# GpSimd's sums and copies moved in its queue, and the seven products of the second FFN layer in a new order

## Chip, cores, metric

Each run uses one core of a Trainium2 chip. The metric is the device time of one execution in microseconds; medians of several runs are quoted.

## The reference

Attention with a threshold (8 batches, 8 heads, 576 positions, head size 64), whose output rows are the input of an FFN with ELU (512 to 2048 to 512):

```python
scores = scale * np.matmul(q, k.transpose(0, 1, 3, 2))
thresh = np.max(scores, axis=-1, keepdims=True) - tau
scores = np.where(scores >= thresh, scores, -1000000000.0)
attn = np.exp(scores - np.max(scores, axis=-1, keepdims=True))
attn = attn / (np.sum(attn, axis=-1, keepdims=True) + 1e-09)
x = np.matmul(attn, v)               # heads side by side: (4608, 512)
h = x @ w_in
g = np.where(h > 0.0, h, np.exp(np.minimum(h, 0.0)) - 1.0)
return g @ w_out
```

## The kernel before

All is float32. Heads go in pairs; a pair has five steps i0 to i4 (i4 holds the last 64 queries of both heads). From pair 7 on, a hand-ordered loop weaves each attention step with `QUOTA` half units of the FFN, so that TensorE (PE) always has matmuls while the other engines do the softmax. An FFN chunk (256 tokens) has 8 units of the first layer and 7 products of the second: 30 halves in ten steps. So the loop repeats every two pairs, called A (odd pairs) and B (even pairs).

The second layer multiplies 2x2 blocks with 7 products instead of 8, so GpSimd (POOL) makes 16 sums `s` of the activations per chunk, and the weights have sums `t`. Products gather in three places X, Y, Z of PSUM (the memory that matmuls write), and VectorE (DVE) adds places and kept tiles afterwards.

```python
def prep_q(pr):                                   # prep_k likewise, with one copy
    qT = qkp.tile([P, S], FP32, name="qT")
    nc.vector.transpose(qT, ...)
    qd = qds[pr % NQD]
    for i in range(2):
        nc.gpsimd.tensor_copy(qd[r, ...], qT[r, MAIN:])     # POOL waits for the transposition
# ...
def exponentials(pr, i, hs):
    nc.vector.tensor_reduce(st["mx"], ...)                  # maximum, reads PSUM
    nc.gpsimd.tensor_scalar(st["nb"], st["mx"], ...)        # bias
    nc.gpsimd.tensor_scalar(st["th"], st["mx"], ...)        # threshold
    nc.scalar.activation(e, ..., AF.Exp, bias=st["nb"])     # one for each head
# masks: DVE, w = (scores >= th) * e, frees the scores' PSUM (one buffer); then 1/sum into rs
# normalize: POOL, w = w * rs
# a first-layer unit ends with exp (ACT), minus one (POOL), elu (DVE)
# ...
QUOTA = ((2, 2), (2, 2), (2, 0), (2, 1), (2, 0))
for n in range(SWITCH, len(steps) + 3):
    # ...
    scores(*step)
    finish_units(after, slice(0, 2))        # exp, minus of the halves of the last step
    exponentials(*step)
    finish_units(after, slice(2, None))     # their elu and other DVE work
    run_extra(1.6)                          # two sums
    turn_squares(*steps[n - 1])
    after = ffn_halves(QUOTA[n % NB][0])
    masks(*step)
    (prep_q if i == 2 else prep_k)(pr + 1)  # only i2, i3
    finish_units(after, slice(0, None))     # exp, minus, elu of these halves
    normalize(*step)
    run_extra(1.6)                          # two sums more
    # ...
    after = ffn_halves(QUOTA[n % NB][1])
```

Each engine is given its instructions in the order of this text, and the timelines below show POOL and DVE run them in that order.

Of the kernel before, what the change touches and what calls it, by code (L numbers as in the profile page):

```python
# [9 lines left out]
FP32 = mybir.dt.float32  # L10
# [3 lines left out]
ALU = mybir.AluOpType  # L14
# [4 lines left out]
def kernel(  # L19
# [10 lines left out]
    nc = tc.nc  # L30
    PSUM = bass.MemoryType.PSUM
    P = 128
    B, H, S, D = q.shape
    DM, DF = moe_w_in.shape
    NC = S // P
    MAIN = NC * P
    TAIL = S - MAIN
# [14 lines left out]
    qkp = ctx.enter_context(tc.tile_pool(name="qkp", bufs=2))  # L52
# [5 lines left out]
    epool = ctx.enter_context(tc.tile_pool(name="epool", bufs=1))  # L58
# [8 lines left out]
    first = ExitStack()  # L67
# [28 lines left out]
    NQD, NVD = 2, 2  # L96
    qds = [const.tile([P, P], FP32, name=f"qd{i}") for i in range(NQD)]
# [51 lines left out]
    raws, pairs = {}, {}  # L149


    def load(pr, parts=("qm", "km", "v")):
        b, j = divmod(pr, NPAIR)
        tiles = raws.setdefault(pr, {})
        for name, src in (("qm", q), ("km", k)):
            if name not in parts:
                continue
            m = tiles[name] = raw.tile([P, S // T, T], FP32, name=name)
            for i in range(2):
                for d in range(2):  # L160
                    r = (2 * i + d) * T
                    nc.sync.dma_start(
                        m[r : r + T],
                        src[b, 2 * j + i].rearrange("(j t) d -> t j d", t=T)[:, :, d * T : (d + 1) * T],
                    )
        if "v" not in parts:
            return
        vm = tiles["vm"] = raw.tile([P, 2, NC, D], FP32, name="vm", bufs=2)
        vd = tiles["vd"] = vds[pr % NVD]
        for i in range(2):  # L170
            vh = v[b, 2 * j + i]
            nc.sync.dma_start(vm[:, i], vh[:MAIN].rearrange("(c p) d -> p c d", p=P))
            r = slice(i * TAIL, (i + 1) * TAIL)
            nc.sync.dma_start(vd[r, r], vh[MAIN:])

    def prep_q(pr):
        qT = qkp.tile([P, S], FP32, name="qT")
        nc.vector.transpose(qT, raws[pr]["qm"].rearrange("p j d -> p (j d)"))
        qd = qds[pr % NQD]
        for i in range(2):  # L180
            r = slice(i * D, (i + 1) * D)
            nc.gpsimd.tensor_copy(qd[r, i * TAIL : (i + 1) * TAIL], qT[r, MAIN:])
        pairs[pr] = [qT, None, qd]

    def prep_k(pr):

        kT = pairs[pr][1] = qkp.tile([P, TAIL + S], FP32, name="kT")
        nc.vector.transpose(kT[:, TAIL:], raws[pr]["km"].rearrange("p j d -> p (j d)"))
        nc.gpsimd.tensor_copy(kT[D:, :TAIL], kT[D:, S:])

    wTs, xts, open_steps, turns = {}, {}, {}, {}

# [161 lines left out]
    PLAIN = 2  # L354
    HM = DM // 2
    gs, ss, cur = {}, {}, {}
    extra = deque()

    def run_extra(budget):
        while extra and extra[0][0] <= budget:  # L360
            cost, _, f = extra.popleft()
            budget -= cost
            f()

    def need_extra(c):
        while any(x[1] <= c for x in extra):
            extra.popleft()[2]()
# [63 lines left out]
    def store(c, i, ot):  # L431
        g, hf = divmod(c, 2)
        t0 = hf * CT + i * P
        if g < B:
            nc.sync.dma_start(out[g * S + t0 : g * S + t0 + P, :], ot)
        else:
            for o in range(2):
                b0 = (t0 // TAIL + o) * S + MAIN
                nc.sync.dma_start(out[b0 : b0 + TAIL, :], ot[o * TAIL : (o + 1) * TAIL])

    def ffn2_plain(c, i, part):
# [10 lines left out]
        def done():  # L452
# [3 lines left out]
            if (c, i) == (PLAIN - 1, 1):  # L456
# [3 lines left out]
        return [lambda: run(0), lambda: run(1)], (done, lambda: None, lambda: None) if 4 * part + 4 == NFT else ()  # L460


    ORDER = ((("g", 0, 0), ("w", 0, 0), "X", True), (("s", 1), ("t", 0), "Y", True), (("s", 0), ("w", 0, 1), "Z", True),
             (("g", 1, 0), ("w", 1, 0), "X", False), (("s", 2), ("t", 1), "Y", False), (("s", 3), ("w", 1, 1), "Z", False),
             (("g", 1, 1), ("t", 2), "Y", False))

    def ffn2(c, m):
        left, right, place, begins = ORDER[m]

        def part(k):  # L470
            if left[0] == "s" or right[0] == "t":
                need_extra(c)
            if begins and k == 0:
                cur[c, place] = psum["f"].tile([P, 512], FP32, name="po", tag="f")[:, :HM]
            for u in range(k * NU // 2, (k + 1) * NU // 2):
                lhs = gs[c][:, u, left[1], left[2]] if left[0] == "g" else ss[c][:, left[1], u]
                if right[0] == "w":
                    rhs = w_out_sb[:, right[1] * NU + u, right[2] * HM : (right[2] + 1) * HM]
                else:
                    rhs = late["t"][:, right[1], u]  # L480
                nc.tensor.matmul(cur[c, place], lhs, rhs, start=(begins and u == 0), stop=(u == NU - 1),  # L481
                                 skip_group_check=True)

        def add(out, x, y):
            nc.vector.tensor_tensor(out, cur[c, x], cur[c, y], ALU.add)

        def kept(name, cols=HM, bufs=1):
            cur[c, name] = epool.tile([P, cols], FP32, name=name[:2], bufs=bufs)
            return cur[c, name]

        def first():
            nc.scalar.copy(kept("s1"), cur[c, "X"])

        def fourth():
            nc.scalar.copy(kept("ot0", DM, 2)[:, :HM], cur[c, "X"])

        def fifth():
            add(kept("ot1", DM, 2)[:, HM:], "Y", "t5")

        def sixth():  # L500
            add(cur[c, "ot0"][:, HM:], "Z", "u2")
            store(c, 0, cur[c, "ot0"])

        def seventh():
            add(cur[c, "ot1"][:, :HM], "Y", "s1")
            store(c, 1, cur[c, "ot1"])

        by_vector = {1: lambda: add(kept("u2"), "Y", "s1"), 2: lambda: add(kept("t5"), "Z", "s1"),
                     4: fifth, 5: sixth, 6: seventh}
        no = lambda: None  # L510
        posts = (no, no, by_vector[m]) if m in by_vector else (first if m == 0 else fourth, no, no)
        return [lambda: part(0), lambda: part(1)], posts

    units = deque()
# [9 lines left out]
    NP = B * NPAIR  # L524
# [10 lines left out]
    def heads_of(i):  # L535
        return [0, 1] if i < NC else [0]
# [33 lines left out]

    def ahead(pr, i):
        if i == 2 and pr + 1 < NP:
            prep_q(pr + 1)
            prep_k(pr + 1)
        if i == 3 and pr + 2 < NP:
            load(pr + 2, ("qm", "km"))
        if i == 3 and pr + 1 < NP and pr:
            load(pr + 1, ("v",))

    load(0)  # L580
    prep_q(0)
    prep_k(0)
    load(1)

    heads = [(pr, i, [h]) for pr, i in steps[:per_seq] for h in heads_of(i)]
# [28 lines left out]
    for n in range(per_seq, SWITCH):  # L614
        pr, i = steps[n]
# [29 lines left out]
    with tc.manual_schedule():  # L645
        after = []
        for n in range(SWITCH, len(steps) + 3):
            step = (*steps[n], heads_of(steps[n][1])) if n < len(steps) else None
            if SWITCH + 1 < n <= len(steps) + 1:
                fetch(*steps[n - 2])  # L650
            if step:
                scores(*step)
            finish_units(after, slice(0, 2))
            if step:
                exponentials(*step)
            finish_units(after, slice(2, None))
            run_extra(1.6)
            if SWITCH < n <= len(steps):
                turn_squares(*steps[n - 1])
            after = ffn_halves(QUOTA[n % NB][0])  # L660
            if step:
                masks(*step)
                pr, i = steps[n]
                if pr + 1 < NP and i in (2, 3):
                    (prep_q if i == 2 else prep_k)(pr + 1)
            finish_units(after, slice(0, None))
            if step:
                normalize(*step)
            run_extra(1.6)
            if n - 3 >= SWITCH:  # L670
                behind(*steps[n - 3])
            if step and pr + 2 < NP and i in (3, 4):
                load(pr + 2, ("qm",) if i == 3 else ("km",))
            if step and pr + 1 < NP and i == 3:
                load(pr + 1, ("v",))
            after = ffn_halves(QUOTA[n % NB][1])
        finish_units(after, slice(0, None))
        xts[B] = xpool.tile([P, KJ, MAIN], FP32, name="xt")
        nc.sync.dma_start(xts[B], xtail.rearrange("j p n -> p j n"))
        push_ffn(B)  # L680
        while pending or units:
            finish_units(ffn_halves(1), slice(0, None))
            run_extra(99)
# [32 lines left out]
```

## Time and profile before

| | before |
|---|---|
| time, median of the first 3 runs | 1466.87 us (1463.84 to 1468.86) |
| loop and tail, from the second step's scores of the loop to the end | 1189.3 us |
| a loop period (ten steps), mostly | 77.08 us |
| PE idle in a period | 1.15 us |

How to read a line: it gives start and length in us, then engine, line of the kernel, operation, tile written and tiles read, and in brackets the engine's idle time before it and who ended it. ACT is ScalarE, PEld the weight loads of PE, SPq the queue that issues DMAs. The tiles are `sc` scores, `mx` their maximum, `nb` bias, `th` threshold, `e` exponentials, `w` masked and normalized weights, `g` FFN activations, `po` products.

The prediction shows lines of waits: who waited for whom, us in total, times, longest. One view more, three of the waits of POOL in the period from 686.78 to 763.86 us (who waited for whom, us in total, times, longest):

```profile
POOL w L246 <- DVE rs L240: 10.0, 6, 3.6
POOL kT L189 <- DVE kT L188: 8.4, 2, 4.2
POOL qd L182 <- DVE qT L178: 6.9, 2, 4.2
```

### The profile page before, as it was taken

The page shows a single profiled execution, that of the slowest core. Times are in us where ns is not written, and L with a number is a line of the kernel's source. Part 1 is how long each engine was busy: PE and PEld are TensorE (multiplying, and loading weights), DVE is VectorE, ACT ScalarE, POOL GpSimd, SP SyncE. Part 2 cuts the span into 40 slices and gives each one's busy share as a digit, 9 for nine tenths or more (in the row PEclk, how much of TensorE's full clock was granted, in tenths as well). Part 3 has the DMA queues.
Part 4 walks back from the last instruction along what each step waited for, and adds up shares of the span by engine and source line. Part 5 has one row for each costly group of instructions (what it writes and reads, how often), then busy time and mean ns, then how long its engine had stood idle before and what let it go on. Part 6 is the DMA issues. An engine that isn't in the chain of part 4 may idle for free.

```text
span 1464.2 us, 20305 instructions
## 1 busy us (share of the span) xinstructions
PE 1396.0 (95%) x6822; PEld 1039.2 (71%) x6822; DVE 875.6 (60%) x1894; ACT 437.7 (30%) x780; POOL 671.3 (46%) x1194
## 2 busy tenths in 40 slices
PE   7988789999999999999999999999999999999998
PEld 4555535647777777777777777777777777888887
DVE  5887665566676766776666767676767674111111
ACT  4665544323232322222232223222322232101100
POOL 4665554446454453535362535353545444323422
PEclk9999999999999999999999999999999999999999
DMA  4244442176767667666676767666767665100000
GB/s 94 71 92 115 116 123 84 50 193 180 185 172 198 172 189 189 188 182 184 178 195 175 188 182 191 181 184 182 193 179 185 187 182 150 44 15 8 8 15 15
DMA packets 298904, 205.45 MB, mean 140 GB/s; under 512 B 206384, under 2 KB 270384, under 8 KB 298800
## 3 DMA queue, kind: packets, MB, share of 16 engines
q1 hardware_dynamic: 298800, 204.15, 52.6%
q8 instruction: 54, 0.88, 0.2%
q14 instruction: 50, 0.41, 0.1%
HBM read 119.87 MB, written 84.21 MB: 139 GB/s over the span
## 4 chain that ended last, share of the span: by engine, by line
PE 71%; DVE 12%; POOL 8%; ACT 3%; issue 3%; DMA 2%; SPq 1%; DVEq 0%; POOLq 0%; ACTq 0%
PE po L481 25%; PE ph L383 25%; PE sc L210 10%; PE pv L337 6%; DVE w L237 4%; POOL w L246 2%; ACT e L225 2%; POOL wtop L141 2%; PE po L449 2%; PE pv L333 2%; DVE mx L220 1%; PE rt L249 1%; DVE x L297 1%; POOL g L394 1%; DVE g L398 1%
## 5 line engine op out<-in xcount | busy, mean ns | idle before, releaser
L383 PE MATMUL ph<-xt,w_in_sb 128*128 128x256 f32 x2304 | 520.4, 382 | 3.2 <-DVE w_in_sb L145 3.2
L383 PEld LDWEIGHTS ph<-xt,w_in_sb 128*128 128x128 f32 x2304 | 432.6, 190 | 83.4 <-issue 21.0
L225 ACT ACTIVATE e<-sc,nb,keep 128x576 f32<-128x576 f32 x288 | 227.8, 829 | 514.6 <-POOL nb L221 513.5
L220 DVE TENSOR_REDUCE mx<-sc 128x2 f32<-128x1152 f32 (+1 forms) x176 | 199.8, 1136 | 188.2 <-PE sc L210 187.9
L246 POOL TENSOR_SCALAR w<-w,rs 128x576 f32<-128x576 f32 x288 | 220.1, 774 | 152.3 <-DVE rs L240 143.2
L237 DVE SCALAR_TENSOR_TENSOR w<-sc,th,e 128x576 f32<-128x576 f32 x288 | 226.8, 815 | 98.3 <-ACT e L225 57.4
L210 PE MATMUL sc<-kT,qT 64*128 64x288 f32 x1024 | 182.1, 441 | 20.1 <-DVE w L237 10.6
L398 DVE SCALAR_TENSOR_TENSOR g<-g,ph 128x512 f32<-128x512 f32 x144 | 97.9, 680 | 150.8 <-POOL g L394 150.8
L297 DVE STREAM_TRANSPOSE x<-w 128x512 f32<-128x512 f32 (+1 forms) x350 | 181.4, 567 | 1.1 <-POOL w L246 0.9
L394 POOL TENSOR_SCALAR g<-g 128x512 f32<-128x512 f32 x144 | 89.9, 625 | 199.2 <-ACT g L391 197.1
L210 PEld LDWEIGHTS sc<-kT,qT 64*128 64x128 f32 x1024 | 100.4, 191 | 87.3 <-issue 53.8
L391 ACT ACTIVATE g<-ph 128x512 f32<-128x512 f32 x144 | 86.0, 597 | 245.0 <-PE ph L383 243.6
L221 POOL TENSOR_SCALAR nb<-mx,nkeep 128x2 f32<-128x2 f32 (+1 forms) x176 | 52.6, 299 | 167.6 <-DVE mx L220 158.4
L481 PE MATMUL po<-w_out_sb,g 128*128 128x256 f32 x512 | 123.6, 383 | 3.4 <-DVE g L398 3.4
L481 PE MATMUL po<-t,s 128*128 128x256 f32 x512 | 118.9, 381 | 0.0
L481 PE MATMUL po<-w_out_sb,s 128*128 128x256 f32 x512 | 118.7, 381 | 0.0
L481 PEld LDWEIGHTS po<-w_out_sb,g 128*128 128x128 f32 x512 | 95.5, 190 | 24.8 <-DVE g L398 7.8
L481 PEld LDWEIGHTS po<-t,s 128*128 128x128 f32 x512 | 96.3, 190 | 17.2 <-issue 4.2
L481 PEld LDWEIGHTS po<-w_out_sb,s 128*128 128x128 f32 x512 | 96.4, 190 | 16.9 <-issue 4.2
L414 POOL TENSOR_TENSOR s<-g 128x256 f32<-128x256 f32 x128 | 93.2, 728 | 14.3 <-DVE g L398 12.9
L337 PE MATMUL pv<-wTb,vm 128*64 128x320 f32 x512 | 76.7, 439 | 0.0
L449 PE MATMUL po<-w_out_sb,g 128*128 128x512 f32 x128 | 62.4, 619 | 4.9 <-DVE w_out_sb L145 4.7
(63 smaller groups left out, 1088.5 us busy)
## 6 DMA issues: line engine op xcount, KB each, us to landing
there<-x SPq DMA_DIRECT2D x500, 144.0 KB, 3.1
wTb<-there SPq DMA_DIRECT2D x75, 576.0 KB, 4.4
wTa<-there SPq DMA_DIRECT2D x50, 576.0 KB, 3.7
qm<-in_q_dram SPq DMA_DIRECT2D x128, 72.0 KB, 2.7
km<-in_k_dram SPq DMA_DIRECT2D x128, 72.0 KB, 3.5
vm<-in_v_dram SPq DMA_DIRECT2D x64, 128.0 KB, 2.5
wst<-in_moe_w_in_dram SPq DMA_DIRECT2D x16, 512.0 KB, 4.2
wst<-in_moe_w_out_dram SPq DMA_DIRECT2D x16, 512.0 KB, 3.8
```

The source lines that it names most:

```text
L210: nc.tensor.matmul(scs[h][:, a, :HALF], qs[r], kT[r, k0 : k0 + HALF], start=True, stop=True)
L220: nc.vector.tensor_reduce(st["mx"][:, cs], src[:, :, :, :HALF], axis=AX.XY, op=ALU.max)
L225: nc.scalar.activation(e, st[h][:, :, :HALF], AF.Exp, bias=st["nb"][:, h : h + 1], scale=keep)
L237: nc.vector.scalar_tensor_tensor(wv, sc[:, :, :HALF], st["th"][:, h : h + 1], e, ALU.is_ge, ALU.mult, accum_out=sm[:, h : h + 1])
L246: nc.gpsimd.tensor_scalar(wv, wv, st["rs"][:, h : h + 1], 1.0, ALU.mult, ALU.mult)
L297: nc.vector.transpose(x[:, :, c0 : c0 + nc_], src.rearrange("p (c g n) -> p g c n", c=nc_, n=T))
L337: nc.tensor.matmul(pv[h * D : (h + 1) * D, g0 * T : g1 * T], vm[:, h, c], wT[:, g0:g1, h * (NC + 1) + c], start=False, stop=(c == NC - 1), ...
L383: nc.tensor.matmul(loc["ph"][:, k], w_in_sb[:, j, ft * P : (ft + 1) * P], xts[g][:, j, hf * CT : (hf + 1) * CT], start=(j == 0), stop=(j = ...
L394: nc.gpsimd.tensor_scalar(loc["g"], loc["g"], 1.0, -1.0, ALU.mult, ALU.add)
L398: nc.vector.scalar_tensor_tensor(loc["g"], loc["g"], 0.0, loc["h"], ALU.min, ALU.max)
L414: nc.gpsimd.tensor_tensor(out, x, y, op)
L481: nc.tensor.matmul(cur[c, place], lhs, rhs, start=(begins and u == 0), stop=(u == NU - 1), skip_group_check=True)
```

## The change

The intent: the bias and the threshold, on which the exponentials wait, shall not stand behind sums or copies in POOL's queue; and since sums then come later, the products that need none shall come first. Cut to its core:

```diff
     def prep_q(pr):
         nc.vector.transpose(qT, ...)
-        for i in range(2):
-            nc.gpsimd.tensor_copy(qd[...], qT[...])
+    def copy_q(pr):          # copy_k likewise
+        for i in range(2):
+            nc.gpsimd.tensor_copy(qd[...], qT[...])
@@ products: left, right, place, begins
-    ORDER = ((g00, w00, X, True), (s1, t0, Y, True), (s0, w01, Z, True), (g10, w10, X, False),
-             (s2, t1, Y, False), (s3, w11, Z, False), (g11, t2, Y, False))
+    ORDER = ((g00, w00, X, True), (g11, t2, Z, True), (g10, w10, X, False), (s1, t0, Y, True),
+             (s0, w01, Z, True), (s2, t1, Y, False), (s3, w11, Z, False))
@@ adds behind the products (DVE; a plain copy is on ACT)
+    0: s1 = X   1: w1 = Z + s1   2: out = X   3: u2 = Y + s1   4: t5 = Z + s1
+    5: out = Y + t5, out = Y + w1   6: out = Z + u2
@@ loop
             finish_units(after, slice(2, None))
-            run_extra(1.6)
+            run_extra(3.0)                      # three sums
             ...
             normalize(*step)
-            run_extra(1.6)
+            (copy_q if i == 2 else copy_k)(pr + 1)      # only i2, i3
```

(Product numbers count from 0, so `u2` is read behind product 3. The old adds are left out; the new ones are one more a chunk, which is why DVE has 1910 instructions after and 1894 before.)

More of the change, by code (lines that the diff above doesn't have):

```diff
@@ L178, in prep_q, with prep_k @@
         nc.vector.transpose(qT, raws[pr]["qm"].rearrange("p j d -> p (j d)"))
-        qd = qds[pr % NQD]
+        pairs[pr] = [qT, None, qds[pr % NQD]]
+    def prep_k(pr):
+        kT = pairs[pr][1] = qkp.tile([P, TAIL + S], FP32, name="kT")
+        nc.vector.transpose(kT[:, TAIL:], raws[pr]["km"].rearrange("p j d -> p (j d)"))
+    def copy_q(pr):
+        qT, _, qd = pairs[pr]
         for i in range(2):
@@ L182, in prep_q, with copy_k, prep @@
             nc.gpsimd.tensor_copy(qd[r, i * TAIL : (i + 1) * TAIL], qT[r, MAIN:])
-        pairs[pr] = [qT, None, qd]
-    def prep_k(pr):
-        kT = pairs[pr][1] = qkp.tile([P, TAIL + S], FP32, name="kT")
-        nc.vector.transpose(kT[:, TAIL:], raws[pr]["km"].rearrange("p j d -> p (j d)"))
+    def copy_k(pr):
+        kT = pairs[pr][1]
         nc.gpsimd.tensor_copy(kT[D:, :TAIL], kT[D:, S:])
+    def prep(pr):
+        for f in (prep_q, copy_q, prep_k, copy_k):
+            f(pr)
     wTs, xts, open_steps, turns = {}, {}, {}, {}
@@ L460, in ffn2_plain @@
         return [lambda: run(0), lambda: run(1)], (done, lambda: None, lambda: None) if 4 * part + 4 == NFT else ()
-    ORDER = ((("g", 0, 0), ("w", 0, 0), "X", True), (("s", 1), ("t", 0), "Y", True), (("s", 0), ("w", 0, 1), "Z", True),
-             (("g", 1, 0), ("w", 1, 0), "X", False), (("s", 2), ("t", 1), "Y", False), (("s", 3), ("w", 1, 1), "Z", False),
-             (("g", 1, 1), ("t", 2), "Y", False))
+    ORDER = ((("g", 0, 0), ("w", 0, 0), "X", True), (("g", 1, 1), ("t", 2), "Z", True), (("g", 1, 0), ("w", 1, 0), "X", False),
+             (("s", 1), ("t", 0), "Y", True), (("s", 0), ("w", 0, 1), "Z", True), (("s", 2), ("t", 1), "Y", False),
+             (("s", 3), ("w", 1, 1), "Z", False))
     def ffn2(c, m):
@@ L470, in part @@
         def part(k):
-            if left[0] == "s" or right[0] == "t":
+            if left[0] == "s":
                 need_extra(c)
-            if begins and k == 0:
+            if right[0] == "t":
+                need_extra(PLAIN)
+            if begins and k == 0 and (c, place) not in cur:
                 cur[c, place] = psum["f"].tile([P, 512], FP32, name="po", tag="f")[:, :HM]
@@ L482, in part, with finals, kept, post @@
                                  skip_group_check=True)
-        def add(out, x, y):
-            nc.vector.tensor_tensor(out, cur[c, x], cur[c, y], ALU.add)
-        def kept(name, cols=HM, bufs=1):
-            cur[c, name] = epool.tile([P, cols], FP32, name=name[:2], bufs=bufs)
-            return cur[c, name]
-        def first():
-            nc.scalar.copy(kept("s1"), cur[c, "X"])
-        def fourth():
-            nc.scalar.copy(kept("ot0", DM, 2)[:, :HM], cur[c, "X"])
-        def fifth():
-            add(kept("ot1", DM, 2)[:, HM:], "Y", "t5")
-        def sixth():
-            add(cur[c, "ot0"][:, HM:], "Z", "u2")
-            store(c, 0, cur[c, "ot0"])
-        def seventh():
-            add(cur[c, "ot1"][:, :HM], "Y", "s1")
-            store(c, 1, cur[c, "ot1"])
-        by_vector = {1: lambda: add(kept("u2"), "Y", "s1"), 2: lambda: add(kept("t5"), "Z", "s1"),
-                     4: fifth, 5: sixth, 6: seventh}
+        def finals(i, cols, x, y):
+            if (c, i) not in cur:
+                cur[c, i] = epool.tile([P, DM], FP32, name="ot", bufs=2), []
+            ot, done = cur[c, i]
+            if y is None:
+                nc.scalar.copy(ot[:, cols], cur[c, x])
+            else:
+                nc.vector.tensor_tensor(ot[:, cols], cur[c, x], cur[c, y], ALU.add)
+            done.append(cols)
+            if len(done) == 2:
+                store(c, i, ot)
+        def kept(name, x, y):
+            cur[c, name] = epool.tile([P, HM], FP32, name=name)
+            if y is None:
+                nc.scalar.copy(cur[c, name], cur[c, x])
+            else:
+                nc.vector.tensor_tensor(cur[c, name], cur[c, x], cur[c, y], ALU.add)
+        lo, hi = slice(0, HM), slice(HM, DM)
+        f, args = ((kept, ("s1", "X", None)), (kept, ("w1", "Z", "s1")), (finals, (0, lo, "X", None)),
+                   (kept, ("u2", "Y", "s1")), (kept, ("t5", "Z", "s1")), (None, ()), (finals, (0, hi, "Z", "u2")))[m]
+        def post():
+            if f:
+                f(*args)
+            else:
+                finals(1, hi, "Y", "t5")
+                finals(1, lo, "Y", "w1")
         no = lambda: None
-        posts = (no, no, by_vector[m]) if m in by_vector else (first if m == 0 else fourth, no, no)
+        posts = (post, no, no) if m in (0, 2) else (no, no, post)
         return [lambda: part(0), lambda: part(1)], posts
@@ L572, in ahead @@
         if i == 2 and pr + 1 < NP:
-            prep_q(pr + 1)
-            prep_k(pr + 1)
+            prep(pr + 1)
         if i == 3 and pr + 2 < NP:
@@ L580 @@
     load(0)
-    prep_q(0)
-    prep_k(0)
+    prep(0)
     load(1)
@@ L668 @@
                 normalize(*step)
-            run_extra(1.6)
+                if pr + 1 < NP and i in (2, 3):
+                    (copy_q if i == 2 else copy_k)(pr + 1)
             if n - 3 >= SWITCH:
```

## The prediction

> **What bounds the kernel now.** I read the page first, then windows, waits, timelines and single records, each time to ask whether TensorE (PE) stands still and for whom.
>
> ```profile
> PE 1396.0 (95%) x6822; PEld 1039.2 (71%) x6822; DVE 875.6 (60%) x1894; ACT 437.7 (30%) x780; POOL 671.3 (46%) x1194
> PE 71%; DVE 12%; POOL 8%; ACT 3%; issue 3%; DMA 2%; SPq 1%; DVEq 0%; POOLq 0%; ACTq 0%
> ```
>
> PE bounds it. The change touches only the hand-scheduled loop (attention of 125 steps woven with the FFN, about 262 to 1228 us) and the FFN tail behind it. The loop repeats every 10 steps: two pairs of heads, called A and B, of five steps i0 to i4, with one FFN chunk of 30 half units. Windows of one loop period and of two pieces of the tail (columns: length, then busy PE, PEld, DVE, ACT, POOL):
>
> ```profile
> 686.78:763.86 77.08, 75.93 (x385) 57.40 (x385) 53.16 (x116) 21.41 (x36) 35.91 (x69) 1.00 0.69 184
> 1303.90:1331.52 27.62, 27.62 (x129) 24.31 (x129) 5.24 (x8) 4.18 (x7) 12.71 (x19) 1.00 0.03 10
> 1331.52:1355.70 24.18, 24.18 (x114) 21.29 (x113) 2.39 (x5) 1.34 (x3) 3.44 (x5) 1.00 0.03 12
> ```
>
> The tail has no PE idle, so nothing is to be won there. A period has 1.15 us. Who makes PE (and its weight loads) wait over ten periods (378 to 1150 us):
>
> ```profile
> PE sc L210 <- DVE w L237: 8.7, 10, 0.9
> PE po L481 <- DVE g L398: 3.4, 11, 0.6
> PEld po L481 <- DVE g L398: 7.8, 11, 1.0
> PEld po L481 <- DVE ot L485: 2.7, 10, 0.3
> ```
>
> So two stalls a period, always at the same place: the scores of step A-i4 wait for the mask of A-i3 (which frees their PSUM), and the last two matmuls of product 0 wait for the last ELU of the chunk. The timelines of POOL, DVE and PE there:
>
> ```profile
> 753.38 0.53 POOL L182 COPY qd<-qT 64x64 f32<-64x64 f32 x2 [2.70 <-DVE qT L178]
> 754.00 0.62 POOL L394 TENSOR_SCALAR g<-g 128x512 f32<-128x512 f32 x1
> 754.60 1.47 POOL L246 TENSOR_SCALAR w<-w,rs 128x576 f32<-128x576 f32 x2
> 756.03 0.72 POOL L414 TENSOR_TENSOR s<-g 128x256 f32<-128x256 f32 x1
> 756.71 0.72 POOL L414 TENSOR_TENSOR s<-g,s 128x256 f32<-128x256 f32 x1
> 757.42 0.26 POOL L221 TENSOR_SCALAR nb<-mx,nkeep 128x2 f32<-128x2 f32 x1
> 755.26 1.35 DVE L220 TENSOR_REDUCE mx<-sc 128x2 f32<-128x1152 f32 x1
> 758.32 1.89 PE L481 MATMUL po<-w_out_sb,g 128*128 128x256 f32 x8
> 761.07 1.21 PE L210 MATMUL sc<-kT,qd 128*128 128x288 f32 x4 [0.86 <-DVE w L237]
> 762.12 1.46 PE L481 MATMUL po<-w_out_sb,g 128*128 128x256 f32 x6
> 763.86 0.70 PE L481 MATMUL po<-w_out_sb,g 128*128 128x256 f32 x2 [0.28 <-DVE g L398]
> ```
>
> POOL stands 2.70 us in front of the copy of q, which waits for DVE's transposition; "minus one" (L394), the normalization (L246) and two sums (L414) queue behind it. The maximum was ready at 756.61, but its bias nb starts only at 757.42. The maximum itself started at 755.26 although the scores ended at 754.83, because the ELU before it on DVE had waited for the late L394.
>
> **What the Trainium skill says.** Perfetto Trace Analysis, Optimization Strategy: "Consistent bubbles" can mean missing SBUF or PSUM. Here the bubble is as consistent (ten times 0.86 to 0.88), but what is late is a queue position, not a buffer. GPSIMD Engine Reference, 3.1: two-input work costs about 2.6 cycles per element; an estimate from that, 256 x 2.6 / 1.2 GHz = 0.55 us, is below the 0.73 us in the trace, which I use. SBUF — State Buffer, the two separate sides: POOL and a VectorE instruction with two SBUF inputs exclude each other. The mask takes 0.82 us beside a sum (at 690.15) and without one (at 696.13), so moving sums beside the masks should cost nothing. Perfetto Trace Analysis, Matmuls: independent groups should rotate through PSUM banks so that evacuation overlaps. The new order reuses Y after one product only; that matters below.
>
> **Part 1: POOL's order.** Sums: instead of two behind the normalization and two behind the threshold, three behind the threshold. A chunk has 16 sums, pushed four at a time; at three a step the queue is empty in B-i0, before product 3 is the first to need them. Copies go behind the normalization. No instruction is added.
>
> *First stall.* PE would be ready for scores A-i4 one issue step after its eighth product matmul. In the last pair (pr = 31), where no q and k are prepared any more but sums still run, the same place looks so:
>
> ```profile
> 1219.13 0.27 POOL L221 TENSOR_SCALAR nb<-mx,nkeep 128x2 f32<-128x2 f32 x1 [0.82 <-DVE mx L220]
> 1221.12 1.89 PE L481 MATMUL po<-w_out_sb,g 128*128 128x256 f32 x8
> 1222.84 1.15 PE L210 MATMUL sc<-kT,qd 128*128 128x288 f32 x4
> ```
>
> 1222.84 - 1221.12 = 1.72, against 761.07 - 758.32 = 2.75: the stall is 1.03 us. Would the chain allow it? After the change: mx at 754.87 to 756.23, nb at 756.33, two exponentials (1.55) at 756.63 to 758.18, two masks (1.56) to 759.84, release 0.15: 759.99, against PE ready at 758.32 + 1.72 = 760.04. It fits by 0.05 us. **Saved 1.03.**
>
> *Second stall.* The last ELU now needs only L394, behind three sums: threshold ends 756.85, sums to 759.1, L394 to 759.8; on DVE it runs behind the transposition of k, 760.9 to 761.6. PE needs it about 1.3 us into product 0, at 762.4. In the records the stalled matmul starts 763.856, the one before 763.195; at the usual spacing of 0.216 that is 0.45 late, and the matmul behind a wait follows at 0.32 instead of 0.22. **Saved 0.55.**
>
> Eleven such places (374 to 1150 us): 11 x 1.58 = 17.4, plus about 0.4 as the first and the one at 995 are longer: 17.8.
>
> *Start of the loop.* PE also stands 1.96 us before scores at 298.20 (same queue, weight sums of 1.27 us in front of nb) and 0.97 at 343.72 (copy of k, normalization, a weight sum in front of nb). The first falls to about 0.25 (chain of 5.2 us after a maximum that starts near 291.3), the second away: 1.75 + 1.0 = 2.8. The 1.6 us at 289.66 stay: only 3.7 us of PE work stand there against a chain of 5.2. **Part 1 in all: 20.6 us.**
>
> **Part 2: the order of products.** Seven products of eight matmul records more or less remain; their spacing is 0.216 in either form. But a new dependence arises: product 3 leaves Y, DVE reads it (u2 = Y + s1), product 5 accumulates onto Y, with product 4 alone between. Product 3 ends early in B-i1; its post is issued behind the masks and the reciprocal of that step. Before, that slot on PE held product 5 on Z, whose reader had long run:
>
> ```profile
> 706.21 0.17 DVE L240 RECIPROCAL rs<-sm 128x2 f32<-128x2 f32 x1
> 706.17 1.89 PE L481 MATMUL po<-w_out_sb,s 128*128 128x256 f32 x8
> ```
>
> The add would start 0.08 behind the reciprocal's start, as at 698.02, take 0.40, and let PE go 0.05 later: 706.21 + 0.08 + 0.40 + 0.05 = 706.75 against 706.17, so 0.58, and 0.10 for the slow second matmul: **0.68 lost**, once a period, in pairs 10, 12, ... 30: 11 x 0.68 = 7.5. That chain begins when the scores of B-i1 end, so POOL's new order does not shorten it. Other reuses have more room: s1 and w1 are read two steps before X and Z are written again; t5 against product 6 is the wait for DVE ot L485 shown above and stays as small. In the tail product 4 gives 3.45 us, enough for a 0.4 us add.
>
> **Sum:** -20.6 + 7.5 = -13.1 us; 1466.9 - 13.1 = **1454 us**, and a period of 77.08 - 1.58 + 0.68 = 76.18.
>
> **Rivals.** (a) No wait on Y, because product 4 or an earlier add covers it: all 20.6 won, 1446. For it: the add is short; against it: the records of B-i1 above. (b) The freed PE runs into the chain at once, as only 0.05 us is left in A-i3: half the first stall stays, 11 x 0.5 = 5.5 us less, 1459.5. For it: the narrow margin; against it: the last pair shows no wait. (c) Sums become late: three in a row (2.2 us) hold up L394 and so the ELU and maximum of the next step, or the last sums miss product 3; at 0.5 to 1 us per period 1460 to 1465. For it: in i0 the sums end at 734.7 and L394 already starts at 734.89; against it: L394 waits there for ACT, not for sums. Only the first chunk after the four last weight sums may carry one sum over.
>
> **Range and chances.** Main story 1454; (a) bounds below with some noise, (b) and (c) above; the three times of before differ by 5 us. Range 1446 to 1462. Over 2% needs under 1437.5, below (a), which takes away every wait I find: chance 0.02. Over 2% slower would need 2.3 us more in each period: 0.02.
>
> **What would show it.** In the profile after: nb of A-i3 within 0.2 us of its maximum, and no PE wait at scores A-i4; no wait for the ELU (L398) in product 0; a new wait of about 0.6 us of product 5 for the add of u2 in each B-i1; periods near 76.2 us; the tail unchanged at 27.6 and 24.2. Periods of 75.5 mean (a); a rest at scores A-i4 (b); waits for sums, or late L394 in A-i0 to A-i2, (c). A loop that isn't shorter at all would prove wrong that POOL's order makes the two stalls.

## The result, and the profile after

1452.01 us (6 runs, 1450.28 to 1457.39) against 1468.15 us (6 runs). Ratios here are the mean time of one kernel's fast runs over that of the other's in the same rounds, so not quite the ratio of the quoted medians: **0.9895, interval 0.9869 to 0.9921**, within 2%, as predicted (1454, range 1446 to 1462).

The page after (busy time; chain that ended last): PE's share of the chain rises from 71% to 82%, DVE and POOL shrink from 12% and 8% to 8% and 4%.

```profile
PE 1391.5 (96%) x6822; PEld 1037.2 (72%) x6822; DVE 878.9 (61%) x1910; ACT 439.7 (30%) x780; POOL 667.7 (46%) x1194
PE 82%; DVE 8%; POOL 4%; ACT 3%; issue 2%; DMA 1%; SPq 0%; POOLq 0%; DVEq 0%; ACTq 0%
```

Windows after: one period, and one chunk's two layers in the tail (length, then busy PE, PEld, DVE, ACT, POOL, and at the end granted clock, DMA share and GB/s):

```profile
697.23:773.44 76.21, 75.80 (x384) 57.39 (x385) 53.34 (x116) 21.61 (x36) 35.69 (x69) 1.00 0.69 188
1237.77:1265.40 27.63, 27.63 (x129) 24.32 (x129) 5.23 (x8) 4.18 (x7) 12.68 (x19) 1.00 0.14 48
1265.40:1289.57 24.17, 24.17 (x113) 21.28 (x113) 2.72 (x6) 1.34 (x3) 3.43 (x5) 1.00 0.03 12
```

The period is 76.21 us (predicted 76.18), with 0.41 us of PE idle left; the tail is as before. Who makes PE and its weight loads wait over ten periods (378 to 1140 us): both old waits are gone, and there is one new, for `u2` (the small one for `t` stood there before, for `ot`).

```profile
PE po L494 <- DVE u L514: 4.1, 10, 0.4
PEld po L494 <- DVE u L514: 8.1, 10, 0.8
PEld po L494 <- DVE t L514: 2.7, 10, 0.3
```

POOL, DVE and PE at step A-i3 (timeline after):

```profile
743.93 1.46 POOL L256 TENSOR_SCALAR w<-w,rs 128x576 f32<-128x576 f32 x2 [0.69 <-DVE rs L250]
745.34 0.52 POOL L190 COPY qd<-qT 64x64 f32<-64x64 f32 x2
747.59 0.27 POOL L231 TENSOR_SCALAR nb<-mx,nkeep 128x2 f32<-128x2 f32 x1 [1.73 <-DVE mx L230]
746.06 1.36 DVE L230 TENSOR_REDUCE mx<-sc 128x2 f32<-128x1152 f32 x1 [1.05 <-PE sc L220]
751.24 1.21 PE L220 MATMUL sc<-kT,qd 128*128 128x288 f32 x4
752.28 1.89 PE L494 MATMUL po<-w_out_sb,g 128*128 128x256 f32 x8
```

The copy no longer waits. The maximum waits for the scores and not for an ELU; the bias follows 0.17 us behind its end (746.06 + 1.36 = 747.42) instead of 0.81. The view gives no idle time in front of the scores of A-i4 or within the eight matmuls of the half product. At B-i1 (DVE and PE, after):

```profile
696.69 0.17 DVE L250 RECIPROCAL rs<-sm 128x2 f32<-128x2 f32 x1
696.77 0.40 DVE L514 TENSOR_TENSOR u<-po,s 128x256 f32<-128x256 f32 x1
693.20 3.62 PE L494 MATMUL po<-w_out_sb,s 128*128 128x256 f32 x16
697.23 1.99 PE L494 MATMUL po<-t,s 128*128 128x256 f32 x8 [0.41 <-DVE u L514]
```

Product 5 could start at 693.20 + 16 x 0.216 = 696.66 (0.216 is the usual spacing) and starts at 697.23, 0.06 behind the end of the add: 0.57 us late.

**Two measures.** The part ahead of the loop differs between profiles: the loop's second step of scores begins between 272.3 and 280.1 us in kernels that do the same up to there. That alone is more than most effects sought. So besides the time I read two numbers from each profile: the *period* (distance from scores A-i4 to the next ones, equal to about 0.02 us but for one stray 0.3) and *loop and tail* (from the second step's scores to the end; the last store alone varies by 0.4, so tenths of it mean little).

### The profile page after: what moved, and what is told of

It reads as the page before. It is cut to its first block, busy times and chain, and to the rows that moved or that the text cites. A ratio compares the mean times of both kernels' runs of the same rounds, so it can differ in the third digit from the quotient of the medians.

```text
span 1449.4 us, 20329 instructions
## 1 busy us (share of the span) xinstructions
PE 1391.5 (96%) x6822; PEld 1037.2 (72%) x6822; DVE 878.9 (61%) x1910; ACT 439.7 (30%) x780; POOL 667.7 (46%) x1194
## 4 chain that ended last, share of the span: by engine, by line
PE 82%; DVE 8%; POOL 4%; ACT 3%; issue 2%; DMA 1%; SPq 0%; POOLq 0%; DVEq 0%; ACTq 0%
PE ph L393 33%; PE po L494 24%; PE sc L220 12%; PE pv L347 8%; DVE w L247 2%; PE pv L343 2%; PE po L459 2%; ACT e L235 2%; POOL wtop L141 2%; DVE mx L230 2%; PE rt L259 1%; POOL w L256 1%; DVE wtop L136 1%; POOL nb L231 1%; DVE w_out_sb L145 1%
## 5 line engine op out<-in xcount | busy, mean ns | idle before, releaser
L494 PE MATMUL po<-t,s 128*128 128x256 f32 x512 | 122.8, 386 | 4.5 <-DVE u L514 4.5
L494 PE MATMUL po<-w_out_sb,g 128*128 128x256 f32 x512 | 117.7, 379 | 0.0
L350 ACT COPY xt<-pv 128x256 f32<-128x256 f32 x64 | 23.8, 372 | 159.3 <-PE pv L347 159.2
```

The source lines that it names most:

```text
L494: nc.tensor.matmul(cur[c, place], lhs, rhs, start=(begins and u == 0), stop=(u == NU - 1), skip_group_check=True)
```

## The experiments

Twelve runs, all correct. They were made in three groups on three chips (e1 to e4; e5, e8, e9, e10; the rest), each beside runs of the kernel before on the same chip (medians 1467.41, 1467.32 and 1466.66). So compare ratios across groups, not times; the change's repeat in the third group gave its period and its loop and tail again. The periods are those of pairs 11 to 29:

| run | time, us | ratio to before | period | loop and tail |
|---|---|---|---|---|
| before | 1468.15 | 1 | 77.08 | 1189.3 |
| after | 1452.01 | 0.9895 | 76.21 | 1175.9 |
| after again | 1453.43 | 0.991 | 76.21 | 1175.9 |
| e1 queue order only | 1447.17 | 0.9865 | 75.54 | 1168.9 |
| e2 product order only | 1473.21 | 1.005 | 77.73 | 1197.7 |
| e3 without the copies' move | 1462.21 | 0.9976 | 77.03 | 1186.3 |
| e4 without the sums' move | 1455.29 | 0.992 | 76.14 | 1176.2 |
| e5 u2 ahead of the masks | 1445.63 | 0.9855 | 75.54 | 1168.5 |
| e8 u2 twice | 1458.08 | 0.9936 | 76.67 | 1181.3 |
| e6 writes of Y further apart | 1446.34 | 0.9866 | 75.53 | 1168.4 |
| e9 copies' move alone | 1448.44 | 0.9863 | 75.47 | 1169.2 |
| e10 e9, add of product 4 sooner | 1449.14 | 0.9871 | 75.33 | 1167.7 |
| e7 e5, t5 sooner | 1443.69 | 0.9836 | 75.40 | 1167.0 |
| e11 e10, weight sums as in the change | 1444.17 | 0.985 | 75.33 | 1166.6 |

The theory was the prediction's: POOL's order takes two waits from each period, the product order adds one. The rivals: the product order is itself a gain or is needed; the sums, not the copies, made the bias late; the new wait has another cause.

### e1 and e2: the two halves of the change apart

e1 is the change with the old `ORDER` and its old adds; e2 is the kernel before with the new ones.

```diff
 e1 (against after)                       e2 (against before)
-    ORDER = new, adds new               -    ORDER = old, adds old
+    ORDER = old, adds old               +    ORDER = new, adds new
```

> GpSimd's new order with the old order of products. Theory (the queue order wins some 20 us, the product order costs some 7.5 by the wait of product 5 on Y): both stalls of A-i3/A-i4 stay away, the wait on u2 is gone too, period 76.21 - 0.68 = 75.53 us, time about 1444.5 (ratio to before 0.984). Rival (the product order is needed because products without sums must come first when sums run three a step): a wait of products for the sums L4xx appears in A-i4 or B-i0, period over 76.2, time above 1452.

> New order of products with GpSimd's old order. Theory: both old stalls stay (1.58 us a period) and the wait on u2 is added, period 77.08 + 0.68 = 77.77, time about 1475.5, 0.5% slower than before. Rival (the product order itself wins): period under 77.08, faster than before.

e1: 75.54 us a period, and from 350 to 1200 us no wait of PE is left; for the sums it has a single 0.4 us wait of a weight load. e2: 77.73, slower than before by 0.5% (interval 1.0035 to 1.0066), with the two old waits and the new one together. In e2's waits (350 to 1200 us, eleven times each):

```profile
PE sc L210 <- DVE w L237: 9.5, 11, 1.0
PE po L483 <- DVE u L503: 4.5, 11, 0.4
PE po L483 <- DVE g L398: 3.4, 11, 0.6
```

So the two halves add up: the queue order is worth 1189.3 - 1168.9 = 20.4 us, and the product order costs 1175.9 - 1168.9 = 7.0 us in the change. In e2 it shows as 8.4 us, of which some 1.7 lie in a stretch of the loop's start (296.41 to 343.60 us, 47.19 us long against 45.52 before) where the granted clock was 0.96 instead of 1.00. That ratio fits the difference, so I leave the 1.7 out. The rival "three sums a step need the new order" falls with e1.

### e3 and e4: copies and sums apart

```diff
 e3 (against after)                       e4 (against after)
     def prep_q(pr):                      -            run_extra(3.0)
         nc.vector.transpose(qT, ...)     +            run_extra(1.6)
+        copy_q(pr)   # prep_k likewise                 ...
     ...                                               normalize(*step)
             normalize(*step)                          (copy_q if i == 2 else copy_k)(pr + 1)
-            (copy_q if ...)(pr + 1)      +            run_extra(1.6)
```

> The change with the copies of q and k back at their old place (in front of the normalization); sums behind the threshold. Theory (the copies that wait for the transpositions are what makes bias and ELU late): in A-i2 the queue still stands until qT is there, the maximum of A-i3 stays late behind the ELU, bias about 756.7 on the old clock: about 0.3 of the first stall and all of the second (0.5) come back, period about 77.0, time about 1463. Rival (the two sums in front of the bias are the cause): period stays 76.2, time 1452.

> The change with the sums back in two pairs (budget 1.6 twice a step); copies behind the normalization. Theory: the normalization then starts about 2 us sooner, the two sums behind it end before the maximum of A-i3 does, so the bias isn't late: period 76.2 as in the change, time 1452 to 1454 (a little lost at the loop's start to weight sums in front of the bias). Rival (sums in front of the bias are the cause): the first stall of about 0.8 to 1.0 us comes back, period about 77.0, time about 1462.

e3's period is 77.03. POOL, DVE and PE at its A-i3 (timeline): the copy again holds the queue for 2.25 us, the maximum starts 0.43 behind the end of the scores (749.03 + 1.24), and the whole wait for the ELU is back. The last line is of its waits from 350 to 1200 us.

```profile
748.83 0.52 POOL L192 COPY qd<-qT 64x64 f32<-64x64 f32 x2 [2.25 <-DVE qT L178]
750.70 1.35 DVE L232 TENSOR_REDUCE mx<-sc 128x2 f32<-128x1152 f32 x1
755.80 1.21 PE L222 MATMUL sc<-kT,qd 128*128 128x288 f32 x4 [0.15 <-DVE w L249]
758.59 0.70 PE L496 MATMUL po<-w_out_sb,g 128*128 128x256 f32 x2 [0.28 <-DVE g L410]
PE sc L222 <- DVE w L249: 0.9, 6, 0.2
```

e4's period is 76.14, even 0.07 less than the change's. In its queue two sums stand ahead of the bias again, but they do no harm (POOL and DVE, timeline): the normalization runs at once behind `rs`, and the sums end at 752.57, before the maximum does (751.36 + 1.36 = 752.72).

```profile
750.56 0.52 POOL L190 COPY qd<-qT 64x64 f32<-64x64 f32 x2
751.17 0.72 POOL L424 TENSOR_TENSOR s<-g 128x256 f32<-128x256 f32 x1
751.85 0.72 POOL L424 TENSOR_TENSOR s<-g,s 128x256 f32<-128x256 f32 x1
752.82 0.27 POOL L231 TENSOR_SCALAR nb<-mx,nkeep 128x2 f32<-128x2 f32 x1 [0.24 <-DVE mx L230]
```

So in the period the move of the copies alone takes both waits away. The sums were late in the kernel before only because a waiting copy stood ahead of them.

The move of the sums is not idle by itself. e2 and e3 differ in it alone, and the period falls from 77.73 to 77.03: with the copies left in their old place, it takes 0.70 of the wait at the scores of A-i4 (9.5 us of such waits in e2, 0.9 in e3) and nothing of the wait for the ELU. The gains do not add: it is part of what the copies' move takes too, and behind that move nothing is left for it in the period. At the loop's start, where the weight sums take 1.27 us each, their move does matter: e4 has waits of 0.68 and 0.32 us there that the change has not.

### e5, e8, e6: the new wait

e5 issues `u2 = Y + s1` ahead of the masks, e8 writes it twice, e6 swaps products 2 and 3 so that two products lie between the writes of Y.

```diff
 e5 (against after)                       e8
     after = ffn_halves(...)              -  tensor_tensor(u2, Y, s1, add)
+    u2 = Y + s1      # when product 3    +  tensor_tensor(u2, Y, s1, add)
     masks(*step)     # was among these   +  tensor_tensor(u2, Y, s1, add)
 e6
-  ... (g11, t2, Z), (g10, w10, X), (s1, t0, Y), (s0, w01, Z), (s2, t1, Y), ...
+  ... (g11, t2, Z), (s1, t0, Y), (g10, w10, X), (s0, w01, Z), (s2, t1, Y), ...
```

> The change, with the add u2 = Y + s1 issued on VectorE ahead of that step's masks instead of behind their reciprocal. Theory (product 5 waits for this read of Y, and nothing else does): the add runs in the idle time in front of the masks, the wait on u2 is gone, period 76.21 - 0.68 = 75.53, time 7.5 us under the change, about 1445; masks about 0.1 later without effect. Rival (the wait is due to the matmuls with t and s themselves, or to the sums): the gap of 0.41 in front of po<-t,s stays, period 76.2.

> The change with the add u2 written twice, one after the other (the same value). Theory (the wait is a plain chain: reciprocal, add, product 5): the gap in front of product 5 grows by one add, 0.35 to 0.41 us, from 0.41 to about 0.8; period about 76.6, time about 4 us over the change. Rival (product 5 waits for the masks or the reciprocal by themselves, the add being beside it): no growth, period 76.2.

> The change with products 2 and 3 swapped: Y is written by products 2 and 5, two products apart, and u2 is added behind the maximum of B-i1. Theory (product 5 waits because only one product lies between the two writes of Y): u2 is done some 3 us before product 5, no wait, period 75.53, time about 1445. Rival (product 5 waits wherever the add stands, or product 2 now comes before its sums): a gap in front of po<-t,s stays.

e5: the add runs in DVE's idle time and product 5 starts without a wait (DVE and PE at B-i1, timeline); period 75.54.

```profile
692.82 0.38 DVE L514 TENSOR_TENSOR u<-po,s 128x256 f32<-128x256 f32 x1
695.31 1.89 PE L494 MATMUL po<-t,s 128*128 128x256 f32 x8
```

e8: the wait grows from 0.41 to 0.87 us, by one add, and the period by 0.46.

```profile
699.76 0.86 DVE L515 TENSOR_TENSOR u<-po,s 128x256 f32<-128x256 f32 x2
700.68 1.56 PE L494 MATMUL po<-t,s 128*128 128x256 f32 x6 [0.87 <-DVE u L515]
```

e6: 75.53, the wait gone by order alone; the add now runs right behind the maximum of B-i1, 4 us before product 5 (DVE, timeline):

```profile
691.16 0.41 DVE L514 TENSOR_TENSOR u<-po,s 128x256 f32<-128x256 f32 x1
```

Three edits of different kinds agree: product 5 waits for that read of Y, behind the reciprocal, and for nothing else. The periods of e5 and e6 are that of e1 (75.54), so nothing else in the product order, its one add more a chunk included, costs time in the period.

### e9, e10, e7, e11: how much is to be had

e9 moves nothing but the copies of the kernel before. e10 and e7 also issue the add behind product 4 ahead of the maximum instead of behind it, since it reads the place that product 6 writes again. e11 is e10 with the weight sums alone as the change has them.

```diff
 e10 (against e9), e7 likewise            e11 (against e10)
-  product 4: posts = (no, no, add)       -  run_extra(1.6)        # behind the threshold
+  product 4: posts = (no, add, no)       +  run_extra(3.0 if weight sums are next else 1.6)
                                          -  run_extra(1.6)        # behind the normalization
                                          +  run_extra(0 if they were else 1.6)
```

> The kernel before with the copies of q and k behind the normalization and nothing else: old products, old sums. Theory (this one move is the gain; the sums' move adds only about 1 us at the loop's start and the product order costs 7.5): period 76.14 - 0.68 = 75.46, time 1447 or so, about 1.4% under before; the small waits of the loop's start (0.3 and 0.7) as in e4. Rival (with the old products the sums must come early, so the old pairs of sums or the earlier sums hold something up): a wait for sums or period of 76 and more.

> As e9, and in addition the add behind product 4 (it reads Y, which product 6 writes again) is issued ahead of the maximum instead of behind it. Theory: the last wait of PE in the loop (PEld for DVE ot, 0.3 us of idle weight load, some 0.13 us of PE time) goes, period about 75.33, 1.4 us under e9. Rival: PE hides this wait already, or the add holds the maximum up: period as e9's or longer.

> As e5, and in addition the add t5 = Z + s1 behind product 4 is issued ahead of the maximum. Theory: as e10 over e9, 0.14 us a period: period 75.54 - 0.14 = 75.40, time about 1.5 under e5, near 1444. Rival: nothing moves, 75.54.

> As e10, with the weight sums of the loop's start all behind the threshold, as the change has them (two there, none behind the normalization), and the other sums in the old pairs. Theory: the two waits of the start (0.68 at scores of the first pair's fourth step, 0.31 at 343) go, period stays 75.33; from the loop's first scores on about 1 us less than e10, 8 to 9 us less than the change; time about 1444, under both kernels. Rival: the weight sums two in a row hold up an ELU or the normalization and the gain is lost.

> The changed kernel once more, on the chip of the three runs beside it, as their measure: period 76.21, time about 1452.

e9 has the period expected (75.47) and is 6.7 us shorter than the change in loop and tail. At its A-i3 (POOL and PE, timeline) the copy no longer waits, and neither do the scores or the half product:

```profile
749.20 0.52 POOL L190 COPY qd<-qT 64x64 f32<-64x64 f32 x2
751.45 0.27 POOL L231 TENSOR_SCALAR nb<-mx,nkeep 128x2 f32<-128x2 f32 x1 [0.24 <-DVE mx L230]
755.16 1.15 PE L220 MATMUL sc<-kT,qd 128*128 128x288 f32 x4
756.15 1.89 PE L492 MATMUL po<-w_out_sb,g 128*128 128x256 f32 x8
```

e10 and e7 take another 0.14 a period; from 350 to 1200 us no PE or weight load of theirs waits for another engine any more, except a few weight loads for a load of v (0.3 us each). e11 is the shortest in loop and tail, 9.3 us under the change run beside it. Its time, 1444.17, is under both kernels (ratio to before 0.985, interval 0.9825 to 0.9875; the change in the same rounds 0.991, 0.9889 to 0.993). e7 was 1443.69; by time the two can't be told apart. e10's time of 1449.14 looks no better than e9's (1448.44), although its loop and tail is 1.5 us shorter; the part ahead of the loop scatters by more (3.8 us between these two profiles), which hides that.

## Why the prediction was right, step by step

- **First stall, 1.03 saved.** Measured 1.01: from the start of the eight product matmuls to the next product matmul behind the scores it is 3.80 us before, 2.78 in the change and 2.72 in e4 and e9 (from single records). So the whole stall was 1.08, and the change leaves 0.07 of it: the bias starts 0.17 behind the end of the maximum, 0.10 in e4 (and in the sum of the prediction). The margin of 0.05 was too small for that, so rival (b) is true in kind, at 0.07 instead of 0.5 us. In the records the late bias waits on two semaphores (DVE's, and POOL's own, which stands behind the copies), in e4 on DVE's alone. The Trainium skill, Perfetto Trace Analysis, Identifying Dependency Chains, says that an instruction that waits for several engines may get a semaphore instruction ahead of it; the trace has one there in the change and in e1 and none in e4 and e9, and the periods of the first two are 0.07 longer than those of the other two in the same product order. That the 0.07 is its cost is likely, not shown by a run of its own.
- **Second stall, 0.55 saved.** Right: all eight matmuls run through, and e3 brings the stall back in full.
- **Start of the loop, 2.8.** The waits at 298.20 and 343.72 (1.96 and 0.97) are both gone, 2.9; the prediction had left 0.25 of the first standing. The 1.6 us in front of the scores of the step before stay, as predicted (1.61, at 288.30).
- **Part 1, 20.6.** e1 measures 20.4. But the prediction charged POOL's order as a whole. e4 and e9 show that in the period the copies' move is enough for all of it, and that the sums' move then counts only at the start; alone it takes 0.70 of the 1.6 us (e3 against e2). Its reading of the queue had the fact in it (2.70 us in front of the copy), yet did not separate the two.
- **Queue or buffer.** The prediction called the late thing "a queue position, not a buffer". For the wait at A-i4 the record does not set the two against each other: the scores have one PSUM buffer, and what PE waits for is its release. e9 shows that the queue order is enough; a second buffer was not tried.
- **Sums beside masks.** The rule that the prediction took from the Trainium skill, SBUF — State Buffer, the two separate sides, is for VectorE instructions with two SBUF inputs. A mask reads its scores from PSUM, so that rule leaves it out, and 0.82 us beside a sum and without one is no test of it.
- **Part 2, 0.68 a period.** Right: 76.21 - 75.54 = 0.67 between the change and e1 or e5. Rival (a) falls. The start 0.08 behind the reciprocal's start, the 0.40 of the add and the 0.06 to PE are in the lines shown, and 0.57 late plus 0.10 for the slow second matmul is the 0.67. (The prediction's sum 706.75 should be 706.74.) In all it forecast 7.5: loop and tail show 7.0, and up to the last scores, without the last store, 7.4.
- **Rival (c), late sums.** From 378 to 1140 us no wait of PE for a sum is in the change.
- **Tail.** 27.63 and 24.17 us, as before.
- **Sum.** -13.1 predicted, -13.4 in loop and tail. No term is off by more than 0.5, so the sum isn't luck. The time fell by 16.1 by the medians; that the rest is the scatter ahead of the loop fits its size, but no run separates it.

Taken together: one part of this change, the copies' move, is worth more than the whole, and the product order is a loss that another place for one add removes.

## What to carry to other kernels

In an in-order queue, look for the instruction that waits and not for the costly ones behind it: moving 0.75 us of copies a pair, which waited for VectorE, was worth some 20 us. Moving four times as much summing took less than half as much from a period when it was done alone, and nothing behind the copies' move. Two moves in one queue can take the same wait, so test each with and without the other. When products are reordered, list each accumulator's reads between two writes and ask where that read stands in its engine's queue, not how short it is. And when the start of a program scatters by more than the effect, measure the period in the trace.

## What the Trainium skill lacked or had wrong

- Perfetto Trace Analysis, Optimization Strategy: the one cause named for a bubble that repeats is that SBUF or PSUM can be short. Here it repeated at 0.86 to 0.88 us and, with the buffers unchanged, went away by queue order alone (e9). An instruction that waits at the head of a queue is missing there as a cause (elsewhere the page does call GPSIMD's queue strict FIFO).
- GPSIMD Engine Reference, 3.1: about 2.6 cycles per element for two inputs. The sums agree in slope: 0.73 us at 256 columns and 1.27 at 512, so 0.54 / 256 x 1.2 GHz = 2.5 cycles. The section has no figure for GPSIMD's fixed cost of an instruction, which is needed for sizes like these: some 0.19 us by these lengths (0.73 - 0.54), 0.14 by the distance of starts in the change (0.69 and 1.23 us).
- On no page that I read: what a second semaphore wait costs (bias 0.17 instead of 0.10 us behind its maximum, if that is the cause), and that behind a wait the second matmul of 128x256 follows at 0.32 us instead of 0.216.
